# Pooled attention, then a gated product: x @ w1 and x @ w2 by one level of Strassen's scheme, in two passes over the batches

## The chip, the cores and the metric

The kernel runs on one core of one Trainium2 chip. A core has TensorE (PE, the matrix unit, with its weight loads shown apart as PEld), VectorE (DVE), ScalarE (ACT), GpSimd (POOL) and SyncE (SP), which here issues all DMAs. Each engine works through its own instructions in order and waits for others at semaphores. The metric is the device time of one execution in microseconds (us); lower is better. Matmuls write to PSUM, which has eight banks of 128 x 512 float32.

## What is computed

```python
def _attn_ref(q, k, v):                     # q, k, v: 8 batches, 8 heads, 576 rows, 64 columns, float32
    k_p = k.reshape(B, H, 72, 8, D).mean(axis=3)
    v_p = v.reshape(B, H, 72, 8, D).mean(axis=3)
    scores = matmul(q, k_p.T) / sqrt(D)
    attn = softmax(scores)
    return matmul(attn, v_p)

def _moe_ref(x, w1, w2, w3, w_out):         # x: 4608 x 512 (heads side by side); w1, w2: 512 x 1024
    a = x @ w1                              # w3: 1024 x 1024; w_out: 1024 x 512; the weights are float64
    b = x @ w2
    return (a * b @ w3) @ w_out             # 4608 x 512, float32
```

Both kernels compute w3 @ w_out first, once, call it W (1024 x 512), and then (a * b) @ W for the tokens.

## The kernel before

The order of all work is written out by hand. Each piece is entered in a plan with a step number (`at(kind, k, fn, ...)`), the plan is sorted by step and, inside a step, by kind (L loads, P work after a matmul, M matmuls of the large products, A matmuls of the attention), and the pieces are issued in that order. Since every engine runs in order, the plan is also the order on each engine's queue.

Weights come as float64, read as pairs of int32. `high` (ACT) and `low`, `conv_b` (DVE) put a float32 together from the two words; `conv_c` sets its sign with ACT's Sign and a product on POOL. Every operand of a large product is split in a rounded part and the rest, `hi` and `lo` (`split`: ACT copies, DVE or POOL subtracts), and each product is done in three passes, hi*hi, hi*lo and lo*hi (`PASSES`).

*Prologue.* For 16 blocks of w3 and 8 of w_out: load, convert, transpose w3 on PE (`w_turn`), split, and multiply (`w_mm`, L571) into W. Beside the second half of this stand the attention of the first tokens and, behind it, the conversion of w1 and w2 in 16 blocks of 512 x 128 (`w12_conv` to `w12_split`), which go into the cells that w3 and w_out leave free.

*Main loop.* Tokens go in 12 chunks of 384 (m). For each of 8 column blocks j of w1 and w2: `a_mm` and `b_mm`, each 12 matmuls (4 blocks of the inner dimension by 3 passes, L510) of 384 columns, `a_post` (ACT copies a from PSUM), `b_post` (DVE multiplies a by b, L530; ACT rounds, L531), `g_lo` (DVE, the rest, L536), and one j later `out_mm`, 9 matmuls of 512 columns (L545) that add to three banks o0 to o2. After the last j `out_post` copies the three banks and stores them.

*Attention.* While chunk m is multiplied, chunk m + 1 goes through attention, spread over m's steps: `load_q` and DVE's transpose (L287); k and v pooled over 8 rows by three additions on POOL (`pool_tree`, L347 to L349); scores (`s_mm`, L389); minima and exponentials (`soft1`: L405, L407, L410 and L411, or the form with ACT's accumulator, L415); normalisation (`soft2`, L424 to L427); copies of the columns left over beyond 128 (`soft3`, L436, L438); PE transposes of the weights (L449, L459) and their splits (L471, L472); the product with v (`av_mm`, L484 to L487), and its split into x's two parts (`av_post`, L495, L496).

PSUM: one bank each for a and b, three for the output, three for attention (`patt`).

Of the kernel before, what the change touches and what calls it, by code (L numbers as in the profile page):

```python
# [29 lines left out]
):  # L30

# [27 lines left out]
    xp = ctx.enter_context(tc.tile_pool(name="xp", bufs=2))  # L59
    p1 = ctx.enter_context(tc.tile_pool(name="p1", bufs=1))  # L60
    p2 = ctx.enter_context(tc.tile_pool(name="p2", bufs=2))
    stp = ctx.enter_context(tc.tile_pool(name="stp", bufs=4))
    osp = ctx.enter_context(tc.tile_pool(name="osp", bufs=3))
    pacc = ctx.enter_context(tc.tile_pool(name="pacc", bufs=1, space=PSUM))
    patt = ctx.enter_context(tc.tile_pool(name="patt", bufs=3, space=PSUM))


    ident = cp.tile([P, P], F32, name="ident")
    kbd = [cp.tile([P, NPR, 2 * KP], F32, name=f"kbd{i}") for i in range(2)]
    vbd = [[cp.tile([P, NPR, P], F32R, name=f"vbd{i}_{s}") for s in range(2)] for i in range(2)]  # L70
    VR = [cp.tile([P, NPR, P], F32R, name=f"VR{i}") for i in range(2)]
# [10 lines left out]
    for i in range(2):  # L82
        nc.gpsimd.memset(kbd[i], 0.0)
        for s in range(2):
            nc.gpsimd.memset(vbd[i][s].bitcast(F32), 0.0)
        nc.gpsimd.memset(VR[i].bitcast(F32), 0.0)
# [3 lines left out]

    def raw_cell(i):
        return cp.tile([P, 1024], I32, tag=f"c{i}", name="raw")

    def hl_cell(i):
        t = cp.tile([P, 2, 512], F32R, tag=f"c{i}", name="hl")
        return t[:, 0], t[:, 1]

    def W_cell(s, i, dt):
        return cp.tile([P, DM], dt, tag=f"W{s}_{i}", name="Wc")

    raw, w3t, wo, w12, W = {}, {}, {}, {}, {}
    FREED = (8, 0, 9, 1, 10, 2, 11, 3, 12, 4, 13, 5, 14, 6, 15, 7)
    w1r, w2r, w3r, wor = (w.bitcast(I32) for w in (moe_w1, moe_w2, moe_w3, moe_w_out))
    stage = {}
    NS = 2 * NJ

    def st_tile(shape):  # L110
        return stp.tile(shape, F32, tag="st", name="st")

    def load_wo(j):
        raw["wo", j] = raw_cell(8 + j)
        nc.sync.dma_start(out=raw["wo", j], in_=wor[j * P:(j + 1) * P, :])

    def load_w3(s):
        h, j = divmod(s, NJ)
        raw["w3", s] = raw_cell(s % 4)
# [4 lines left out]
    def load_w12(j, w):  # L124
        raw["w12", j, w] = raw_cell(FREED[2 * j + w])
        nc.sync.dma_start(
            out=raw["w12", j, w].rearrange("p (k c) -> p k c", k=NK),
            in_=(w1r, w2r)[w][:, 2 * j * P:2 * (j + 1) * P].rearrange("(k p) c -> p k c", p=P))
# [11 lines left out]
    def conv_a(c, r, z):  # L140
        high(c, z)
        low(c, r)

    def conv_b(r, z):
# [3 lines left out]

    def conv_c(r, z):
        nc.scalar.activation(out=z, in_=z, func=AF.Sign)  # L150
        nc.gpsimd.tensor_tensor(out=f(r), in0=f(r), in1=z, op=ALU.mult)

    def split(src, hi, lo, eng=nc.vector):
        nc.scalar.copy(out=hi, in_=src)
        eng.tensor_tensor(out=lo, in0=src, in1=f(hi), op=ALU.subtract)  # L155

    def w_tiles(s):
        if s == 0:
            stage["wt"] = [t[:, i] for t, x in (
                (p1.tile([P, x, 512], I32, tag=tag, name="wt"), x)  # L160
                for tag, x in (("PTh", 3), ("PTl", 3), ("PTr", 1))) for i in range(x)]
        if s < NJ:
            stage["wo", s] = stage["wt"][s % 4], f(stage["wt"][4 + s % 3])
        stage["w3", s] = W_cell(0, 4 + s % 4, I32), W_cell(1, 4 + s % 4, F32)

    def w_block(v):
# [10 lines left out]
        if old:  # L177
            s = v - 2
            nc.vector.tensor_tensor(out=wo[s][1], in0=f(stage["wo", s][0]), in1=f(wo[s][0]), op=ALU.subtract)  # L179
        if new:  # L180
            if v > 0:
                low(raw["wo", v], ro)
# [5 lines left out]
        if new:  # L188
            conv_c(r3, z3)
            if v == 0:  # L190
                low(raw["wo", v], ro)
# [543 lines left out]
```

## Time and profile before

| what | value |
|---|---|
| median of 3 runs | 829.68 us (829.64 to 829.82) |
| the profiled execution | 831.34 us, span 829.4 us, mean granted TensorE clock 0.974 |
| DMA moved | 62.63 MB: 52.43 MB read from HBM, 9.44 MB written |
| first matmul of the main loop | at 107.3 us |
| chunk 1 begins, last chunk begins | at 186.3 us and 773.0 us |

The profile is that of one execution. "Busy" is the time in which an engine had an instruction in it; rows of instructions name the line of the kernel, the engine, the operation and the tiles (out<-in). The span is cut in 40 slices on the page, and each digit is a slice's busy share in tenths. Two waits are the longest of those on PE's products: ACT for a (L520) 160.5 us and DVE for b (L530) 122.4 us; in both the waiting engine is not the one that sets the pace.

### The profile page before, as it was taken

The page shows a single profiled execution, that of the slowest core. Times are in us where ns is not written, and L with a number is a line of the kernel's source. Part 1 is how long each engine was busy: PE and PEld are TensorE (multiplying, and loading weights), DVE is VectorE, ACT ScalarE, POOL GpSimd, SP SyncE. Part 2 cuts the span into 40 slices and gives each one's busy share as a digit, 9 for nine tenths or more (in the row PEclk, how much of TensorE's full clock was granted, in tenths as well). Part 3 has the DMA queues.
Part 4 walks back from the last instruction along what each step waited for, and adds up shares of the span by engine and source line. Part 5 has one row for each costly group of instructions (what it writes and reads, how often), then busy time and mean ns, then how long its engine had stood idle before and what let it go on. Part 6 is the DMA issues. An engine that isn't in the chain of part 4 may idle for free.

```text
span 829.4 us, 11726 instructions
## 1 busy us (share of the span) xinstructions
PE 785.1 (95%) x4320; PEld 726.7 (88%) x4320; DVE 460.9 (56%) x881; ACT 304.6 (37%) x759; POOL 255.9 (31%) x274
## 2 busy tenths in 40 slices
PE   6787788699999999999999999999999999999998
PEld 5466677699999999999999999999999999999997
DVE  7997899856537337446345356365373374462112
ACT  5756656633224323323234233232243233232111
POOL 5586679630700810205203603007008102000000
PEclk8979988999999999999999999999999999999999
DMA  9896882004403403017014230044034030100101
GB/s 330 205 207 160 243 196 56 1 1 105 106 1 88 106 19 75 1 39 151 22 46 88 77 76 1 1 105 106 2 84 109 20 76 1 39 1 1 39 0 39
DMA packets 113160, 62.63 MB, mean 76 GB/s; under 512 B 80208, under 2 KB 96848, under 8 KB 113104
## 3 DMA queue, kind: packets, MB, share of 16 engines
q1 hardware_dynamic: 113104, 61.89, 29.7%
q8 instruction: 34, 0.56, 0.3%
q14 instruction: 22, 0.18, 0.1%
HBM read 52.43 MB, written 9.44 MB: 75 GB/s over the span
## 4 chain that ended last, share of the span: by engine, by line
PE 80%; DVE 9%; DMA 5%; issue 4%; ACT 2%; SPq 1%; DVEq 0%
PE o L545 23%; PE a L510 23%; PE b L510 23%; PE att L389 4%; DMA raw<-in_moe_w_dram 3%; PE att L449 2%; DVE Wc L138 2%; PE att L486 1%; PE att L485 1%; PE att L487 1%; PE att L484 1%; PE att L459 1%; DMA raw<-in_moe_w_out_dram 1%; ACT E L415 1%; DVE R L438 1%
## 5 line engine op out<-in xcount | busy, mean ns | idle before, releaser
L510 PE MATMUL a<-xT,hl 128*128 128x384 f32 x1152 | 223.3, 342 | 0.0
L510 PE MATMUL b<-xT,hl 128*128 128x384 f32 x1152 | 221.9, 340 | 0.0
L510 PEld LDWEIGHTS a<-xT,hl 128*128 128x128 f32 x1152 | 205.2, 191 | 5.1 <-POOL hl L155 0.3
L510 PEld LDWEIGHTS b<-xT,hl 128*128 128x128 f32 x1152 | 200.6, 190 | 0.0
L545 PE MATMUL o<-Wc,gh 128*128 128x512 f32 x576 | 183.6, 400 | 0.0
L530 DVE TENSOR_TENSOR a<-b,a 128x384 f32<-128x384 f32 x96 | 53.1, 553 | 122.4 <-PE b L510 122.4
L545 PEld LDWEIGHTS o<-Wc,gh 128*128 128x128 f32 x576 | 105.1, 189 | 17.3
L545 PE MATMUL o<-Wc,gl 128*128 128x512 f32 x288 | 114.0, 396 | 0.0
L520 ACT COPY a<-a 128x384 f32<-128x384 f32 x96 | 46.0, 479 | 179.5 <-PE a L510 160.5
L347 POOL TENSOR_TENSOR st<-st 72x512 f32<-72x512 f32 (+1 forms) x53 | 74.3, 1402 | 121.8 <-DMA st<-in_k_dram 121.1
L531 ACT CAST gh<-a 128x384 fp32r<-128x384 f32 x96 | 49.1, 512 | 148.5 <-DVE a L530 148.3
L360 POOL TENSOR_TENSOR vbd<-vm,vbd 64x256 fp32r<-64x256 f32 x16 | 13.8, 862 | 248.4 <-ACT vbd L359 245.0
L536 DVE TENSOR_TENSOR gl<-a,gh 128x384 fp32r<-128x384 f32 x96 | 60.3, 628 | 36.2 <-ACT gh L531 35.8
L496 DVE TENSOR_TENSOR xT<-att,xT 128x384 fp32r<-128x384 f32 x48 | 26.7, 557 | 75.1 <-ACT xT L495 75.1
L545 PEld LDWEIGHTS o<-Wc,gl 128*128 128x128 f32 x288 | 54.1, 188 | 12.5
L411 DVE TENSOR_REDUCE sm<-E 128x4 f32<-128x288 f32 (+1 forms) x70 | 31.6, 451 | 46.3 <-ACT E L410 46.3
L389 PE MATMUL att<-kbd,qT 128*128 128x144 f32 (+1 forms) x320 | 53.3, 290 | 1.2 <-ACT E L415 1.2
L571 PE MATMUL o<-hl 128*128 128x512 f32 x144 | 45.2, 452 | 9.1 <-DVE hl L179 8.9
L405 DVE TENSOR_REDUCE mx<-att 128x4 f32<-128x288 f32 (+1 forms) x80 | 35.9, 449 | 30.3 <-PE att L389 30.3
L410 ACT ACTIVATE E<-E 128x288 f32<-128x288 f32 (+1 forms) x70 | 31.1, 445 | 54.3 <-DVE E L407 54.2
L389 PEld LDWEIGHTS att<-kbd,qT 128*128 128x128 f32 (+1 forms) x320 | 47.5, 182 | 2.3 <-ACT E L415 1.7
L571 PEld LDWEIGHTS o<-hl 128*128 128x128 f32 x144 | 30.1, 216 | 17.8 <-DVE hl L179 11.3
(90 smaller groups left out, 927.8 us busy)
## 6 DMA issues: line engine op xcount, KB each, us to landing
raw<-in_moe_w_dram SPq DMA_DIRECT2D x32, 512.0 KB
st<-in_k_dram SPq DMA_DIRECT2D x32, 288.0 KB
out_dram<-ob SPq DMA_DIRECT2D x35, 256.0 KB
st<-in_v_dram SPq DMA_DIRECT2D x32, 256.0 KB
qs<-in_q_dram SPq DMA_DIRECT2D x128, 48.0 KB
raw<-in_moe_w_out_dram SPq DMA_DIRECT2D x8, 512.0 KB
st<-in_v_dram SPq DMA_DIRECT2D x64, 64.0 KB
qs<-in_q_dram SPq DMA_DIRECT2D x128, 24.0 KB
```

Source lines behind the costliest of these rows:

```text
L347: nc.gpsimd.tensor_tensor(out=t[:, :, 0:4], in0=t[:, :, 0:4], in1=t[:, :, 4:8], op=ALU.add)
L389: nc.tensor.matmul(out=ps[:nt, 2 * KP * j:2 * KP * (j + 1)], lhsT=qT[n][:, pr, off:off + nt], rhs=kbd[b % 2][:, pr], start=True, stop=True,)
L405: nc.vector.tensor_reduce(out=mx[:nt, hs], in_=sv, axis=AX.X, op=ALU.min)
L410: nc.scalar.activation(out=E[:nt, hs], in_=E[:nt, hs], func=AF.Exp, scale=-1.0)
L411: nc.vector.reduce_sum(out=sm[:nt, hs], in_=E[:nt, hs], axis=AX.X)
L510: nc.tensor.matmul(out=o, lhsT=w12[j, w][sw][:, kt * P:(kt + 1) * P], rhs=x[sx][:, kt], start=(i == 0), stop=(i == 3 * NK - 1))
L520: nc.scalar.copy(out=a, in_=gt[m, j][:, :CH])
L530: nc.vector.tensor_tensor(out=g, in0=ps[:, :CH], in1=g, op=ALU.mult)
L531: nc.scalar.copy(out=gh, in_=g)
L536: nc.vector.tensor_tensor(out=gl, in0=g, in1=f(gh), op=ALU.subtract)
L545: nc.tensor.matmul(out=oacc[m][t], lhsT=(gh, gl)[sg][:, c], rhs=W[j][sw], start=(j == 0 and i == 0), stop=(j == NJ - 1 and i == 2))
L571: nc.tensor.matmul(out=wacc[h][it], lhsT=w3t[s][sa][:, it * P:(it + 1) * P], rhs=wo[j][sb], start=(j == 0 and i == 0), stop=(j == NJ - 1 a ...
```

## The change

Nearly all functions of the kernel are rewritten; the attention's arithmetic, the three passes and the prologue's w3 @ w_out are kept.

*Seven products for eight.* x of one batch (576 tokens, transposed: 512 x 576) is cut in 2 x 2 blocks (256 x 288), and so is each quarter of the columns: in a pass, w1 and w2 have 512 columns each, as two quarters of 256, so that `qq` runs over (w1, w2) twice. One level of the Strassen-Winograd scheme gives the 2 x 2 result from 7 products of blocks. Each is a group of 6 matmuls of 288 columns (`grp_mm`). Before, a batch's same quarter was 8 such products.

*Sums of weights*, once in a pass (`w12_sums`, `w12_split`): four sums per quarter on DVE, and splits of all seven operands.

*Sums of x*, once for each batch and pass (`x_sum1`, `x_sum2`: four subtractions on DVE of 128 x 576; `x_split`: seven splits, ACT and DVE).

*Sums of products* (`grp_post`): ACT copies the first group; DVE adds the others from PSUM, seven additions in a quarter. For w1 the four results go to the tile `g`; for w2 they are added up in small tiles and POOL multiplies them into `g`.

*Two passes.* Iterations 0 to 7 are the batches with the first half of the columns, 8 to 15 the same with the second half. x of each batch is kept in DRAM (`xd`, `x_store`, `x_load`), partial outputs too (`pd`); in the second pass `out_post` adds them. Half of W waits in DRAM as well (`wbd`). The conversion of w1's and w2's second half lies in iteration 7.

*Output.* `out_mm` now comes after the four quarters, in tiles of 128 tokens, two halves each. Odd batches have 5 tiles, even ones 4: the last 64 tokens of an even batch stay in `g` and go with the next (`SHIFT`).

*Steps.* An iteration has 24: groups in the first 14, two a step; from step 13 on x's sums and splits for the next iteration, the splits of g, and the output halves from step 14.

*Other edits.* Attention goes by batch (5 tiles of up to 128 tokens) and x is left unsplit by it (`av_post` only copies). `conv_c` is gone; `conv_b` has a second DVE instruction for the sign. All pooling of k and all splits of w1 and w2 have one engine (POOL and DVE). kbd, vbd and VR have one copy instead of two. PSUM: four banks for groups (`pset`), four for attention and output (`patt`).

```diff
     def conv_b(r, z):
...
         nc.vector.scalar_tensor_tensor(
             out=r, in0=z.bitcast(I32), scalar=3, in1=r, op0=ALU.logical_shift_left, op1=ALU.bitwise_or)
-
-    def conv_c(r, z):
-        nc.scalar.activation(out=z, in_=z, func=AF.Sign)
-        nc.gpsimd.tensor_tensor(out=f(r), in0=f(r), in1=z, op=ALU.mult)
+        nc.vector.scalar_tensor_tensor(
+            out=r, in0=z.bitcast(I32), scalar=-2 ** 31, in1=r, op0=ALU.bitwise_and, op1=ALU.bitwise_or)
...
+    def w12_sums(ph, qq):
...
+        add(s1, a21, a22)
+        sub(s2, s1, a11)
+        sub(s3, a11, a21)
+        sub(s4, a12, s2)
...
+    def x_sum1(i):
+        t = stage["xs", i] = [p2.tile([P, 2, HS], F32, tag="qs", name="xs") for _ in range(2)]
+        sub(t[0], xb(i, 0, 1), xb(i, 0, 0))
+        sub(t[1], xb(i, 1, 1), t[0])
+
+    def x_sum2(i):
+
+        t = stage["xs", i]
+        sub(t[0], xb(i, 1, 1), xb(i, 0, 1))
+        sub(t[1], xb(i, 1, 0), t[1])
+
+    def x_split(i, n):
+        t = p1.tile([P, 2, 2, HS], F32R, tag=f"xo{XN.index(n)}", name="xo")
+        xo[i, n] = t[:, 0], t[:, 1]
...
+        split(src, *xo[i, n])
...
+    GROUPS = (("A11", "B11"), ("S2", "T2"), ("S1", "T1"), ("S3", "T3"),
+              ("A12", "B21"), ("S4", "B22"), ("A22", "T4"))
...
+    def grp_mm(i, qq, n):
...
+        wn, xn = GROUPS[n]
+        ps = acc[i, qq, n] = pset.tile([P, 512], F32, tag=f"p{(7 * qq + n) % 4}", name="ps")
+        w, x = sw[i // B, qq, wn], xo[i, xn]
+        for j, (kt, (a, b)) in enumerate((kt, ps) for kt in range(2) for ps in PASSES):
+            nc.tensor.matmul(out=ps[:, :HS], lhsT=w[a][:, kt * P:(kt + 1) * P], rhs=x[b][:, kt],
+                             start=(j == 0), stop=(j == 5))
+
+    def grp_post(i, qq, n):
+
+        o = acc.pop((i, qq, n))[:, :HS]
+        w2 = qq % 2
+
+        def res(jj, t2, u, into):
+            d = quad(i, qq, jj, t2)
+            if w2:
+                add(tmp[into], u, o)
+                mul(d, d, tmp[into], nc.gpsimd)
+            else:
+                add(d, u, o)
+
+        if n == 0:
...
+            nc.scalar.copy(out=tmp["m1"], in_=o)
+        elif n == 1:
+            add(tmp["u2"], tmp["m1"], o)
+        elif n == 2:
+            add(tmp["u4"], tmp["u2"], o)
+        elif n == 3:
+            add(tmp["u3"], tmp["u2"], o)
+            res(1, 1, tmp["u4"], "u5")
+        elif n == 4:
+            res(0, 0, tmp["m1"], "m1")
+        elif n == 5:
+            res(0, 1, tmp["u4"], "u4")
+        else:
+            res(1, 0, tmp["u3"], "u3")
...
+    def out_post(i, t):
         ob = osp.tile([P, DM], F32, tag="ob", name="ob")
...
+        ps = oacc.pop((i, t))
+        if i < B:
+            if t % 2:
+                nc.vector.tensor_copy(out=ob, in_=ps)
             else:
...
+                nc.scalar.copy(out=ob, in_=ps)
+            nc.sync.dma_start(out=pd[tile_no(i, t)], in_=ob)
+            return
+        add(ob, part.pop((i, t)), ps)
...
+    for i in range(NIT):
+        m0 = M0 + IT * i
+        for qq in range(4):
+            for n in range(7):
+                g = 7 * qq + n
+                k = m0 + g // 2
+                at("M", k + 0.1 * (g % 2), grp_mm, i, qq, n)
+                at("P", k + 1 + 0.01 * (g % 2), grp_post, i, qq, n)
+        nt = len(out_tiles(i))
+        order = [(0, 0), (1, 0), (0, 1), (1, 1)] + [(t, h) for t in range(2, nt) for h in range(2)]
+        for x, (t, h) in enumerate(order):
+            k = m0 + OUT0 + x
+            at("M", k, out_mm, i, t, h)
+            if t < 2:
+                at("P", k - 1 + 0.13 if h == 0 else k + 0.13, g_split, i, t, slice(2 * h, 2 * h + 2))
+            elif h == 0:
+                at("P", k - 0.87, g_split, i, t, slice(0, 4))
+            if h:
+                at("P", k + 1.05, out_post, i, t)
+            if i >= B and h == 0:
+                at("L", k - 3, part_load, i, t)
+        if i + 1 < NIT:
+            plan_x(i + 1, m0 + OUT0 - 1)
+        if i + 1 < B:
+            at("L", m0 + OUT0 + 8, x_store, i + 1)
+        if B <= i + 1 < NIT:
+            at("L", m0 - 2, x_load, i + 1)
```

More of the change, by code (lines that the diff above doesn't have):

```diff
@@ new lines, in w12_split @@
+    def w12_split(ph, qq):
+        own = [cell(i, [P, 2, 512], F32R, "sw") for i in OWN[qq]]
+        if qq % 2 == 0:
+            stage["both"] = cell(BOTH[qq // 2], [P, 2, 2, 256], F32R, "sw")
+        s12, r0, s34, a22 = stage.pop(("sums", ph, qq))
+        for i, (t, src) in enumerate(zip(own, (r0, s12, s34))):
+            for o in range(2):
+                c = slice(256 * o, 256 * o + 256)
+                sw[ph, qq, NAMES[2 * i + o]] = t[:, 0, c], t[:, 1, c]
+            split(src, t[:, 0], t[:, 1])
+        both = stage["both"][:, :, qq % 2]
+        sw[ph, qq, "A22"] = both[:, 0], both[:, 1]
+        split(a22, *sw[ph, qq, "A22"])
@@ new lines, with rows, soft_act, load_q @@
+    NT = (S + P - 1) // P
+    def rows(t):
+        return min(P, S - t * P)
+    def soft_act(n, t):
+        return n == 0 or t in (1, 3)
+    qT, km, vm = {}, {}, {}
+    def load_q(n, pr):
+        t = stage["q", n, pr] = p2.tile([P, S // 32, 32], F32, tag="qs", name="qs")
+        for par in range(2):
+            for db in range(2):
+                g = 2 * par + db
+                nc.sync.dma_start(
+                    out=t[32 * g:32 * g + 32],
+                    in_=q[n, 2 * pr + par, :, 32 * db:32 * db + 32].rearrange("(n t) e -> t n e", t=32))
@@ L357, in prep_v2 @@
         r = slice(64 * par, 64 * par + 64)
-        hi, lo = (vbd[b % 2][s][r, :, D * par:D * par + D] for s in range(2))
-        nc.scalar.copy(out=hi, in_=vm[b][r])
-        nc.gpsimd.tensor_tensor(out=lo, in0=vm[b][r], in1=f(hi), op=ALU.subtract)
+        hi, lo = (vbd[s][r, :, D * par:D * par + D] for s in range(2))
+        split(vm[b][r], hi, lo, nc.gpsimd)
     def prep_vr(b):
@@ L471, in pt_post @@
[L471 to L472 removed]
+        hi, lo = (x[:, :, t * P:t * P + nt] for x in PT[n][:2])
+        split(pv[:, :, :nt], hi, lo)
     def ptr_post(n, t):
[L475 to L488 removed]
@@ L550, in out_post @@
-    def out_post(m, t):
-        ob = osp.tile([P, DM], F32, tag="ob", name="ob")
-        r0 = m * CH + t * P
-        last = m == NCH - 1 and t == 2
-        for i in range(2 if last else 1):
-            c = slice(i * DM // 2, (i + 1) * DM // 2) if last else slice(0, DM)
-            if t == 1 or i == 1:
-                nc.vector.tensor_copy(out=ob[:, c], in_=oacc[m][t][:, c])
-            else:
-                nc.scalar.copy(out=ob[:, c], in_=oacc[m][t][:, c])
-            nc.sync.dma_start(out=out[r0:r0 + P, c], in_=ob[:, c])
+        nt = rows(t)
@@ new lines, in out_tiles, with g_split @@
+    def out_tiles(i):
+        b = i % B
+        r = [(SHIFT + P * t, [(b * S + SHIFT + P * t, P)]) for t in range(4)]
+        if b % 2 == 0:
+            return r
+        return [(0, [((b - 1) * S, SHIFT), (b * S, SHIFT)])] + [(c + SHIFT, x) for c, x in r]
+    oacc, part = {}, {}
+    def g_split(i, t, js):
+        if js.start == 0:
+            G[i, t] = [p2.tile([P, 4, P], F32R, tag=tag, name=tag) for tag in ("gh", "gl")]
+        c = out_tiles(i)[t][0]
+        h, l = G[i, t]
+        split(G["g"][:, js, c:c + P], h[:, js], l[:, js])
@@ new lines, in out_mm, with tile_no, part_load @@
+    def out_mm(i, t, half):
+        if half == 0:
+            oacc[i, t] = bank()
+        for j in (2 * half, 2 * half + 1):
+            for n, (a, b) in enumerate(PASSES):
+                nc.tensor.matmul(
+                    out=oacc[i, t], lhsT=G[i, t][a][:, j], rhs=W[i // B, j][b],
+                    start=(j == 0 and n == 0), stop=(j == 3 and n == 2))
+    def tile_no(i, t):
+        return 9 * (i % B // 2) + 4 * (i % 2) + t
+    def part_load(i, t):
+        if "part" not in stage:
+            stage["part"] = p1.tile([P, 4, DM], F32, tag="PTh", name="part")
+        part[i, t] = stage["part"][:, t % 4]
+        nc.sync.dma_start(out=part[i, t], in_=pd[tile_no(i, t)])
```

606 lines of the change are left out of this document (283 added, 323 removed).

## The prediction

> **What bounds the kernel now.** I read the page's busy shares first, then its 40 slices, then the stretches of the program one by one, then TensorE's timeline and the groups of instructions by shape.
>
> ```profile
> span 829.4 us, 11726 instructions
> PE 785.1 (95%) x4320; PEld 726.7 (88%) x4320; DVE 460.9 (56%) x881; ACT 304.6 (37%) x759; POOL 255.9 (31%) x274
> PE   6787788699999999999999999999999999999998
> DVE  7997899856537337446345356365373374462112
> PE 80%; DVE 9%; DMA 5%; issue 4%; ACT 2%; SPq 1%; DVEq 0%
> ```
>
> The kernel has two parts. Over the first nine slices VectorE (DVE) is as full as anything; from the ninth on TensorE (PE) never rests, and VectorE is near half. The cuts below are the first product with w1 (107.3), the starts of chunk 1 (186.3) and of the last chunk (773).
>
> ```profile
> 0.00:107.30 107.30, 80.57 (x367) 64.44 (x368) 93.77 (x128) 66.07 (x162) 70.85 (x70) 0.87 0.86 231
> 107.30:186.30 79.00, 65.40 (x349) 60.37 (x348) 66.03 (x92) 42.34 (x117) 53.30 (x43) 0.91 0.24 53
> 186.30:773.00 586.70, 586.70 (x3337) 553.30 (x3336) 290.50 (x643) 186.23 (x461) 131.79 (x162) 1.00 0.23 55
> 773.00:829.40 56.40, 52.48 (x274) 48.57 (x272) 10.65 (x19) 9.98 (x20) 0.00 (x0) 0.98 0.08 28
> ```
>
> Columns: stretch, length, then busy PE, weight loads, DVE, ACT, POOL, then clock, DMA share, GB/s. Ten chunks take 586.7 us, all of it PE at clock 1.00: 58.67 each. DVE does 29.05 us of work in each, POOL 13.2. So a saved matmul is worth its time there, and added DVE work is free as long as it stays under PE's time. That limit is what this prediction turns on.
>
> **What PE gains.** The rows give the rate at three widths, and the price of attention work slipped in between:
>
> ```profile
> 699.39 0.27 PE L484 MATMUL att<-PTh,vbd 128*128 128x192 f32 x1
> ...
> 699.83 2.27 PE L510 MATMUL a<-xT,hl 128*128 128x384 f32 x12
> ...
> 724.41 0.65 PE L389 MATMUL att<-kbd,qT 128*128 128x144 f32 x4
> 724.81 2.34 PE L510 MATMUL b<-xT,hl 128*128 128x384 f32 x12
> 726.99 0.65 PE L389 MATMUL att<-kbd,qT 128*128 128x144 f32 x4
> 729.57 0.60 PE L449 MATMUL att<-ident,E 128*128 128x128 f32 x4
> 730.00 0.38 PE L459 MATMUL att<-ident,R 128*128 128x128 f32 x2
> 730.14 2.35 PE L510 MATMUL a<-xT,hl 128*128 128x384 f32 x12
> ...
> 804.39 2.27 PE L510 MATMUL a<-xT,hl 128*128 128x384 f32 x12
> 806.50 2.24 PE L510 MATMUL b<-xT,hl 128*128 128x384 f32 x12
> 808.58 0.62 PE L545 MATMUL o<-Wc,gh 128*128 128x512 f32 x2
> 810.67 1.58 PE L510 MATMUL a<-xT,hl 128*128 128x384 f32 x8
> ```
>
> From start to start: 24 matmuls of 384 columns take 4.19 us, 0.1746 each; 9 of 512 take 2.09, 0.2322 each; four of 192 (L484 to L487) take 0.44, 0.11 each, which lies above the line through the other two (0.088), so a floor shows there. 288 columns are not in the trace; they lie between 0.11 and 0.1746, and the line of the two wide ones gives 0.131. I take that.
>
> - Before, one j costs 6.28 us (804.39 to 810.67), a chunk 50.24, twelve 602.9. Attention adds 58.67 - 50.24 = 8.43 to a chunk, eleven times 92.7. Together 695.6.
> - After, there are 16 iterations (8 batches, 2 passes) of 28 groups of 6 matmuls: 0.79 a group, 22.1 an iteration. The output has 4 or 5 tiles of 12 matmuls of 512, 2.79 each, 12.5 on average. One iteration is 34.6 us.
> - Attention of one batch: 10 score halves at 0.49 (0.40, and 0.10 that the next group loses: 2.18 for 2.08), 5 tiles of transposes at 0.65, 8 products at 4 x 0.131, 0.3 for k: 12.6 us, seven times in the loop.
> - After in all: 16 x 34.6 + 7 x 12.6 = 641.8. PE's work falls by 54 us.
>
> A rule of the Trainium skill would price this differently: TensorE: Matmul & The Clock Gate, section Back-to-back issue gap, gives columns/2.4 GHz plus 2.5 ns, an estimated 0.1225 us at 288. The trace disagrees at 384, where that rule gives 0.1625 and the rows 0.1746. By the rule the 2688 group matmuls would be 24 us cheaper.
>
> **What the other engines pay.** Rows of groups by shape (busy us, mean ns):
>
> ```profile
> L407 DVE TENSOR_TENSOR E<-att,mx 128x288 f32<-128x288 f32 x42 | 19.2, 457 | 1.4
> L427 DVE TENSOR_TENSOR E<-E,sm 128x576 f32<-128x576 f32 x24 | 19.1, 797 | 0.8
> L427 DVE TENSOR_TENSOR E<-E,sm 96x576 f32<-96x576 f32 x16 | 15.0, 936 | 0.5
> L405 DVE TENSOR_REDUCE mx<-att 128x4 f32<-128x288 f32 x48 | 21.6, 451 | 21.6 <-PE att L389 21.6
> L472 DVE TENSOR_TENSOR PTl<-att,PTh 128x512 fp32r<-128x512 f32 x24 | 16.5, 689 | 10.7 <-ACT PTh L471 10.5
> L287 DVE STREAM_TRANSPOSE qT<-qs 128x384 f32<-128x384 f32 x48 | 27.2, 567 | 0.0
> L146 DVE SCALAR_TENSOR_TENSOR wt<-wt 128x512 int32<-128x512 int32 x8 | 5.4, 680 | 0.3 <-ACT wt L133 0.3
> L426 DVE RECIPROCAL sm<-sm 128x8 f32<-128x8 f32 x24 | 4.9, 203 | 0.8
> L347 POOL TENSOR_TENSOR st<-st 128x512 f32<-128x512 f32 x24 | 32.5, 1355 | 0.5
> L348 POOL TENSOR_TENSOR st<-st 128x256 f32<-128x256 f32 x24 | 19.2, 801 | 1.9
> L349 POOL TENSOR_TENSOR km<-st 72x128 f32<-72x128 f32 x29 | 16.4, 566 | 2.3
> ```
>
> Back to back, a VectorE instruction starts before the row of the one ahead of it ends:
>
> ```profile
> 161.94 0.68 DVE L146 SCALAR_TENSOR_TENSOR wb<-wb 128x512 int32<-128x512 int32 x1
> 162.54 0.55 DVE L530 TENSOR_TENSOR a<-b,a 128x384 f32<-128x384 f32 x1
> 163.01 0.44 DVE L405 TENSOR_REDUCE mx<-att 96x4 f32<-96x288 f32 x1
> 163.49 0.45 DVE L407 TENSOR_TENSOR E<-att,mx 96x288 f32<-96x288 f32 x1
> ```
>
> Starts lie 0.60, 0.47 and 0.48 apart. An independent one costs its row less 0.08 on a full queue; one that needs the one ahead (L407 after L405) pays 0.04 on top. The Trainium skill (VectorE: DVE Perf Modes, The DRAIN you can't avoid) has the next instruction wait until the pipe is empty; the trace shows no such full wait. With whole durations the sum below would be 6 us more in each attention iteration.
>
> One iteration of the first pass with attention, on DVE:
> - group sums: 7 additions a quarter from PSUM (u2, u4, u3 and four results), 28 x (0.457 - 0.08) = 10.5;
> - the combinations of x and their splits: 4 + 7 instructions of 576 columns at 0.758 (L427's median, below) - 0.08 = 7.4;
> - splits of g, 0.61 for 512 columns and 0.34 for 256: 2.9; two copies of partial results: 1.2;
> - attention: 4 transposes of 576 columns 2.75; 10 minima and 6 subtractions 6.7; 3 sums of 576 columns 2.0; 5 normalisations (0.20 + 0.24 + 0.68) 5.5; 10 small subtractions 1.45; 5 splits 2.8: 21.2.
>
> Sum 43.2, against PE's 47.2 for the same iteration and DVE's 1.5 x 29.05 = 43.6 for a batch in 88 us before. So DVE gets as much work in roughly half the time. POOL has 7 pooling trees at about 2.75 (L347, L348, L349), 4 of small work, and 8 new products of 288 columns at about 0.87 (between L348 and L347): 30 us of some 52, 58%, where before it was 131.79 of 586.7, 22%. That costs DVE time:
>
> ```profile
> L427 DVE TENSOR_TENSOR E<-E,sm x40: 753/758/1700, 73.1 to 739.8; 128x576 f32<-128x576 f32 x24, 96x576 f32<-96x576 f32 x16
> L536 DVE TENSOR_TENSOR gl<-a,gh x96: 514/558/2014, 118.1 to 822.5; 128x384 fp32r<-128x384 f32 x96
> L146 DVE SCALAR_TENSOR_TENSOR wb<-wb 128x512 int32<-128x512 int32 x16 | 20.8, 1301 | 0.9 <-ACT wb L133 0.8
> ```
>
> Minimum, median, maximum: two SBUF inputs usually cost 0.758 and at worst 1.700. The 40 take 34.1 us, 12% over the median's 30.3; L146 beside POOL's conversions averages 1.301 where it costs 0.680 without them. Scaled from 22% to 58%, 17.2 us of such work an iteration grows by a third, 6 us: 49. Bounds: 0, and 17 if everything doubles as L146 did.
>
> That is above PE's 47.2, and the work is not even. The output's ten steps also hold the x work, g's splits, copies and two softmax tiles: 18 us on DVE, 21.5 with contention, against PE's 15.5 (12.5, two tiles of scores, one of transposes). The 14 group steps hold the group sums, q's transposes and three softmax tiles: DVE 27, PE 32. Were each part bound by its own engine, it would be 53.6; four PSUM banks let PE run about 3 us ahead. I take 52. ScalarE did 18.6 a chunk, 28 a batch (186.23 over ten chunks); with x's and g's splits for those it loses it stays near that, and hides.
>
> **The sum.**
> - Prologue, on DVE: 24 weight conversions at 1.64 (the sign is now a second L146, 0.68, instead of ACT and POOL) 39.4, their splits 14.4, six conversions of w1/w2 with sums and splits 21, attention 0 16.2, x 7.4, the rest 4: 103, with contention 9, first data 4: 116; DVE was 93.77 of 107.3 busy before, with less POOL beside it now I take 93%: 126 (118 to 138). Before, the stall-free equivalent is 829.4 - 695.6 - 6 of tail = 128. So nothing is gained.
> - Iteration 0: 49, 0.4 of the next attention 8.5, the last quarter of the weights 7: 65 (58 to 70).
> - Iterations 1 to 5: 52 each, 260 (48 to 60 each).
> - Iteration 6 holds half an attention and falls to PE: 44.
> - Iteration 7: 22.2 as above, and the second half of w1/w2: 8 conversions 13.2, 16 sums 6.2, splits 8.7, contention 2.5: 53.
> - Second pass, 8 times: PE's 22.1 for groups; output 12.5 on PE, 13.0 on DVE (7.4, 2.9, additions of partial results 2.7); and a handoff of 2, since the last quarter's sum, POOL's product and both splits stand behind x work while PE has 2.8 of other output: 37 (35.5 to 39). Sum 296, less 2 for the last, which prepares no x.
> - Tail 6.
>
> 126 + 65 + 260 + 44 + 53 + 294 + 6 = 848 of span, 18 over the 829.4 of before. The profiled execution took 831.34 in all, 1.9 more than its span and 0.2% over the median of 829.68; the two about cancel, so 848 stands for the median too.
>
> New transfers (x 1.18 MB out and in, partial results alike) are put at nothing: DMA is 0.23 busy in the loop, and a read of x is issued 15 steps before its use. Without that cover each read costs 5 us (at the 231 GB/s of the first row), 40 in all. SP issues in order, so a partial result that waits for its copy holds back k and v loads, and POOL behind them; that belongs to the slower rival.
>
> **The rivals.**
> 1. Faster: DVE keeps under PE. If contention stays below 4 us an iteration, every iteration is PE's 47.5: 118 + 60 + 5 x 47.5 + 44 + 50 + 8 x 35.5 - 2 + 6 = 798. For it: 43.2 is below 47.2, and L407, with an input in PSUM, averages 0.457 and 0.45 alone (163.49), so the group sums should not stretch. Against: it needs DVE over 90% busy in order, with ACT and POOL between its steps. It decides at about 50 us an iteration, with the second pass at 36; below that the change wins.
> 2. Slower still: POOL blocks DVE for whole instructions. 37 instructions with only SBUF operands meet POOL 58% of the time and wait half of 1.36: 15 us, so 58 to 60 an iteration, 75 for the first, 39 in the second pass: 130 + 75 + 5 x 59 + 48 + 58 + 310 + 6 = 922 at the full price, 885 at half. L536's 2.014 (0.558 plus one L347) speaks for it, its median against it. The Trainium skill states just that (SBUF — State Buffer, Who interferes with whom): the later of the two fully blocks.
> 3. The change doesn't do what it says: 288 columns cost what 384 do. 2688 x 0.043 = 116 us more on PE, 58 of them in the second pass and on the path; in the first PE's 47 become 54, 2 over my 52: some 920. The 192 rows speak against it.
>
> **How the numbers follow.** Within 0.2% (1.7 us) is what a measurement of this kernel cannot tell from no change. Mine 0.50, its own range 822 to 878; the first rival 0.21 (798 to 828); between them within 0.2%: 0.04; the second 0.22 (878 to 925); the third 0.03. Faster 0.21, same 0.04, slower 0.75. The range 808 to 900 leaves out the lower part of the first rival and the upper part of the second.
>
> **What would show it.** Group matmuls 0.131 apart, and DVE over 90% busy between about 126 and 545 us with PE below 95%, then PE full again with DVE near 80%. L427's mean above 1.0 us would show the contention. Wrong if iterations 1 to 5 take PE's 47 us, or if PE waits for POOL's products or for x's read instead of DVE.

## The result, and the profile after

The changed kernel takes 1083.27 us (median of 4 runs, 1082.66 to 1083.32) where the kernel before takes 829.75 on the same chip: a ratio of 1.304 (1.3025 to 1.3059). It is 30% slower. The prediction had the sign right and missed the size by far: 848 was forecast, with 900 as the upper end.

The page of the kernel after: length, busy time of the engines, TensorE, VectorE and the granted clock in 40 slices, and the chain that ended last by engine.

```profile
span 1081.4 us, 13558 instructions
PE 840.3 (78%) x4704; PEld 722.0 (67%) x4704; DVE 761.9 (70%) x1415; ACT 358.1 (33%) x1033; POOL 309.8 (29%) x354
PE   7467436667868878788796896759789898898898
DVE  7756795885786867867778773995775765756654
PEclk9868768778989889799798997869899898898989
PE 39%; DVE 38%; ACT 11%; issue 5%; DMA 4%; POOL 2%; SPq 2%; DVEq 0%; ACTq 0%; POOLq 0%
```

Before, TensorE's line was a row of nines from the ninth slice on, and the chain was 80% TensorE. Now no engine stays full: TensorE is busy 78% of the span and VectorE 70%, and the chain goes to and fro between them, 39% and 38%. So look at the stages: prologue, iteration 0, iterations 1 to 5, 6, 7, and the second pass with the tail, then without its last iteration. Columns: stretch, length, then busy PE, weight loads, DVE, ACT, POOL, then clock, DMA share, GB/s.

```profile
0.00:160.30 160.30, 90.71 (x422) 72.78 (x423) 118.38 (x202) 68.21 (x195) 44.70 (x55) 0.80 0.59 162
160.30:262.40 102.10, 68.89 (x352) 59.38 (x352) 72.51 (x137) 38.91 (x130) 37.84 (x44) 0.78 0.25 68
262.40:612.30 349.90, 281.74 (x1648) 242.41 (x1647) 264.57 (x504) 140.24 (x466) 159.92 (x175) 0.89 0.38 91
612.30:665.60 53.30, 47.56 (x285) 41.19 (x284) 35.17 (x75) 20.75 (x62) 6.56 (x8) 0.90 0.07 26
665.60:737.00 71.40, 47.38 (x229) 39.70 (x228) 54.86 (x105) 22.73 (x44) 7.61 (x8) 0.78 0.38 127
737.00:1081.40 344.40, 303.96 (x1777) 266.58 (x1775) 216.42 (x393) 67.24 (x138) 53.16 (x64) 0.92 0.23 79
737.00:1040.40 303.40, 267.16 (x1550) 233.32 (x1549) 195.89 (x352) 62.46 (x127) 46.57 (x56) 0.92 0.24 80
```

| stage | predicted | measured | more |
|---|---|---|---|
| prologue | 126 | 160.3 | 34 |
| iteration 0 | 65 | 102.1 | 37 |
| iterations 1 to 5 | 260 (52 each) | 349.9 (70.0 each) | 90 |
| iterations 6, 7 | 44, 53 | 53.3, 71.4 | 9, 18 |
| second pass and tail | 300 | 344.4 | 44 |

Every term is short, and in each stage the two loaded engines have gaps. In iterations 1 to 5 VectorE's work is 264.57 / 5 = 52.9 us each, where the forecast had 49, and TensorE's busy time 56.3, where it had 47.2; the iteration takes 70.0. Part of TensorE's excess goes with the granted clock, 0.89 here and 1.00 in the chunks before; how much is not separated. An iteration falls into a part with the groups and a part with the output. Here are one of the first pass (402.10) and one of the second (866.10), groups first:

```profile
402.10:438.40 36.30, 32.33 (x236) 30.25 (x235) 27.32 (x63) 13.47 (x48) 13.05 (x17) 1.00 0.55 102
438.40:472.30 33.90, 24.46 (x102) 18.15 (x101) 26.38 (x41) 14.84 (x46) 19.02 (x20) 0.80 0.22 81
866.10:888.40 22.30, 22.30 (x169) 22.30 (x168) 12.85 (x29) 2.48 (x6) 4.26 (x6) 1.00 0.29 109
888.40:911.60 23.20, 18.55 (x62) 13.12 (x62) 15.60 (x23) 6.42 (x12) 2.32 (x3) 0.78 0.29 88
```

In the second pass the groups run as a row of matmuls with nothing between: 168 of them in 22.30 us, 0.133 each. What the change promised for TensorE is there in full. The output part lasts 19 to 23 us where TensorE has 11 to 14 of work, and in the first pass 32 to 34 where the forecast gave it 15.5. The output parts hold most of the loss: the x work of the next iteration and g's splits stand there on VectorE. What TensorE waits for in the iteration at 402.10, the two longest (us in total, times, longest us), where `gh` is the rounded part of g, from ScalarE, and `gl` the rest, from VectorE:

```profile
PE att L604 <- DVE gl L94: 4.7, 4, 1.9
PE att L604 <- ACT gh L151: 4.4, 4, 2.1
```

All of these lie in the output part, and they are 9.1 of TensorE's 13.8 us of waits in that iteration.

What the instructions cost, from the groups by shape (busy us, mean ns), and the same instructions one by one in the first pass's output part, on DVE and on POOL:

```profile
L546 PE MATMUL ps<-xo,sw 128*128 128x288 f32 x2688 | 392.8, 305 | 13.7 <-DVE u L97 9.0
L97 DVE TENSOR_TENSOR u<-u,ps 128x288 f32<-128x288 f32 x224 | 94.6, 449 | 32.7 <-PE ps L546 31.6
L94 DVE TENSOR_TENSOR xo<-xs,xo 128x576 fp32r<-128x576 f32 x64 | 61.0, 952 | 10.5 <-ACT xo L151 8.4
L94 DVE TENSOR_TENSOR xs<-x 128x576 f32<-128x576 f32 x32 | 39.0, 1219 | 0.6
L100 DVE TENSOR_TENSOR E<-E,sm 128x576 f32<-128x576 f32 x32 | 24.6, 770 | 1.1
```

```profile
445.25 1.72 DVE L94 TENSOR_TENSOR xs<-x 128x576 f32<-128x576 f32 x1
...
448.10 1.00 DVE L94 TENSOR_TENSOR xo<-xs,xo 128x576 fp32r<-128x576 f32 x1
449.02 1.83 DVE L94 TENSOR_TENSOR xo<-x,xo 128x576 fp32r<-128x576 f32 x1
450.77 0.94 DVE L94 TENSOR_TENSOR gl<-g,gh 128x256 fp32r<-128x256 f32 x1
```

```profile
444.57 2.99 POOL L97 TENSOR_TENSOR st<-st 128x512 f32<-128x512 f32 x2
448.45 2.99 POOL L97 TENSOR_TENSOR st<-st 128x512 f32<-128x512 f32 x2
```

The x work lies right beside POOL's pooling trees: 1.0 to 1.83 where the forecast took 0.758. The softmax's product on full tiles (L100, once L427), most of which lies elsewhere, is at 0.770. The additions that read PSUM (L97) are not stretched at all: the 25 of them that overlap the trees' additions take at most 0.455. Contention is a matter of place, and an average over the iteration by POOL's busy share could not see it. This is the second rival's mechanism. Whether it is also the second rival's *time* is what the experiments ask.

### The profile page after: what moved, and what is told of

It reads as the page before. It is cut to its first block, busy times and chain, and to the rows that moved or that the text cites. A ratio compares the mean times of both kernels' runs of the same rounds, so it can differ in the third digit from the quotient of the medians.

```text
span 1081.4 us, 13558 instructions
## 1 busy us (share of the span) xinstructions
PE 840.3 (78%) x4704; PEld 722.0 (67%) x4704; DVE 761.9 (70%) x1415; ACT 358.1 (33%) x1033; POOL 309.8 (29%) x354
## 2 busy tenths in 40 slices
DMA packets 124869, 102.60 MB, mean 95 GB/s; under 512 B 79744, under 2 KB 96128, under 8 KB 122752
## 4 chain that ended last, share of the span: by engine, by line
PE 39%; DVE 38%; ACT 11%; issue 5%; DMA 4%; POOL 2%; SPq 2%; DVEq 0%; ACTq 0%; POOLq 0%
PE ps L546 22%; PE att L604 13%; DVE xs L94 6%; DVE xo L94 6%; ACT E L425 4%; DVE gl L94 4%; DVE u L97 3%; ACT xo L151 2%; DVE mx L418 2%; POOL st L97 2%; DVE wr L147 2%; DVE wr L145 1%; DVE E L100 1%; DVE PTl L94 1%; DVE sw L94 1%
## 5 line engine op out<-in xcount | busy, mean ns | idle before, releaser
L546 PE MATMUL ps<-xo,sw 128*128 128x288 f32 x2688 | 392.8, 305 | 13.7 <-DVE u L97 9.0
L546 PEld LDWEIGHTS ps<-xo,sw 128*128 128x128 f32 x2688 | 377.6, 196 | 20.1 <-DVE u L97 9.9
L604 PE MATMUL att<-W,gh 128*128 128x512 f32 x576 | 212.9, 455 | 60.8 <-ACT gh L151 60.8
L100 POOL TENSOR_TENSOR g<-g,u 128x288 f32<-128x288 f32 x96 | 79.3, 840 | 541.1 <-DVE u L97 541.1
L604 PEld LDWEIGHTS att<-W,gh 128*128 128x128 f32 x576 | 119.4, 218 | 97.7 <-ACT gh L151 77.9
L604 PE MATMUL att<-W,gl 128*128 128x512 f32 x288 | 132.7, 461 | 46.1 <-DVE gl L94 46.1
L97 POOL TENSOR_TENSOR st<-st 72x512 f32<-72x512 f32 (+1 forms) x112 | 136.2, 1216 | 87.1 <-DMA st<-in_k_dram 52.1
L97 DVE TENSOR_TENSOR u<-u,ps 128x288 f32<-128x288 f32 x224 | 94.6, 449 | 32.7 <-PE ps L546 31.6
L604 PEld LDWEIGHTS att<-W,gl 128*128 128x128 f32 x288 | 61.5, 214 | 83.6 <-DVE gl L94 71.0
L94 DVE TENSOR_TENSOR gl<-g,gh 128x256 fp32r<-128x256 f32 (+1 forms) x104 | 71.6, 699 | 29.8 <-ACT gh L151 29.5
L97 DVE TENSOR_TENSOR u<-m,ps 128x288 f32<-128x288 f32 x64 | 29.0, 453 | 61.1 <-PE ps L546 51.6
L151 ACT CAST gh<-g 128x256 fp32r<-128x256 f32 (+1 forms) x104 | 49.5, 486 | 42.4 <-PE att L604 36.6
L97 DVE TENSOR_TENSOR ob<-part,att 128x512 f32<-128x512 f32 x36 | 24.8, 688 | 49.3 <-PE att L604 49.2
```

Of the source, the lines that this page charges most:

```text
L94: eng.tensor_tensor(out=out, in0=a, in1=b, op=ALU.subtract)
L97: eng.tensor_tensor(out=out, in0=a, in1=b, op=ALU.add)
L100: eng.tensor_tensor(out=out, in0=a, in1=b, op=ALU.mult)
L546: nc.tensor.matmul(out=ps[:, :HS], lhsT=w[a][:, kt * P:(kt + 1) * P], rhs=x[b][:, kt], start=(j == 0), stop=(j == 5))
L604: nc.tensor.matmul(out=oacc[i, t], lhsT=G[i, t][a][:, j], rhs=W[i // B, j][b], start=(j == 0 and n == 0), stop=(j == 3 and n == 2))
```

## The experiments

Two readings run through all of them. The first is a sum of work: POOL's trees stretch VectorE's instructions, VectorE is the bound, and time falls with its work. The second is a chain: TensorE, VectorE and ScalarE wait for each other in order (products to VectorE's sums, to g's or x's splits on ScalarE and VectorE, back to TensorE), so their times partly add, and time falls only if a step is taken out of the chain or moved ahead in its queue. All times below are of one execution beside the kernel before on the same chip (830 us) unless an interval is given; two executions of the last version differ by 2.9 us, so small differences are read from the stages and not from the total. "Each" means iterations 1 to 5, which some of the expectations call 2 to 6.

**The x work, later.** The x work stood before g's splits from one step ahead of the output; here it begins 4.2 steps later.

```
-            plan_x(i + 1, m0 + OUT0 - 1)
+            plan_x(i + 1, m0 + OUT0 + 3.2)
```

> x's sums and splits for the next iteration are moved 4.2 steps later in the plan, behind the splits of g for the first two output tiles. Theory of order (x work stands ahead of g's splits on VectorE's queue, PE waits for them and its clock falls): second-pass iterations from 43.3 us to 37, first-pass ones (2 to 6) from 70 to about 62; about 980 us in all. Theory of load (the first pass is as long as VectorE's and POOL's work with its stretching makes it, wherever it stands): second pass the same gain of 45 us, first pass stays at 70; about 1038. If the later splits make the next groups wait instead: 1083.

Measured: 1039.74 us, 1.252 (1.2485 to 1.2557) times the time before. Iterations 1 to 5, the second pass up to its last iteration, and one group:

```profile
262.30:606.30 344.00, 281.99 (x1649) 242.88 (x1647) 237.66 (x504) 139.98 (x466) 146.13 (x175) 0.92 0.39 93
723.30:997.50 274.20, 254.60 (x1550) 228.56 (x1549) 185.90 (x352) 62.20 (x127) 46.48 (x56) 0.98 0.26 86
```

```profile
L94 DVE TENSOR_TENSOR xs<-x 128x576 f32<-128x576 f32 x32 | 25.2, 788 | 0.6
```

Most of the stretching is gone (788 ns instead of 1219), and VectorE's work in iterations 1 to 5 falls by 27 us, 5.4 each. Their time falls by 5.9 us in all, 1.2 each. The total is the one that the theory of load gave (1038), but that theory had the stretching stay wherever the x work stands, and it went. That speaks against a sum of work in the first pass: 5.4 us less on what should be the bound, and little more than a fifth of it comes back. What the stretching costs by itself this does not show, since the later x work also comes later for the next groups (those parts last 36 to 39 us here, 36 to 38 before). In the second pass, where no trees run and the work falls by only 10 us in seven iterations, each falls from 43.3 to 39.2: there g's splits no longer wait behind the x work.

**No x work but the first.** All iterations use the first batch's x.

```
-        w, x = sw[i // B, qq, wn], xo[i, xn]
+        w, x = sw[i // B, qq, wn], xo[0, xn]
...
-            plan_x(i + 1, m0 + OUT0 - 1)
```

> x's sums and splits are left out for all batches but the first, whose operands every batch uses. Theory of order: second pass 35.5 us an iteration, as in the last one, which prepares no x; first pass about 60, close to what x_late gives; about 940 in all. Theory of load: the first pass falls by more than x_late's, by the 10 to 13 us that the work takes, to 57 to 60, while x_late's stays near 70.

Measured: 967.32 us.

```profile
252.60:565.60 313.00, 267.13 (x1649) 234.09 (x1647) 202.43 (x450) 119.42 (x431) 143.44 (x175) 0.96 0.43 102
674.20:924.20 250.00, 245.41 (x1550) 225.15 (x1549) 135.38 (x275) 33.67 (x78) 46.50 (x56) 1.00 0.29 98
```

Without it the second pass is TensorE's, 245.41 of 250.00 at clock 1.00, 35.7 us each, as expected: nearly its whole excess over TensorE's 34.6 is the x work. The first pass falls to 62.6 each, which is above what either theory gave: 7.4 less for 12.4 us less on VectorE, and still 15 us too many.

**No pooling trees.** The first two additions of `pool_tree` are left out.

> Two of the three additions of each pooling tree on POOL are left out (k and v are then pooled over two rows only). Theory of contention (POOL holds VectorE up): VectorE's x splits fall from 1.0 to about 0.76 us each, first-pass iterations from 70 to 62 to 64, prologue 5 us less; about 1020 to 1035. Theory of order: the rows get shorter, but an iteration loses only 2 to 4 us: about 1055 to 1065.

Measured: 1029.54 us; 63.9 each, with the output parts at 29.5 and 27.4, and VectorE's work at 47.0 each:

```profile
240.30:559.60 319.30, 273.68 (x1649) 235.67 (x1647) 235.12 (x504) 141.15 (x466) 77.22 (x105) 0.94 0.40 100
```

6.1 us less each, 12.5 in iteration 0, and the first group comes 9.6 us earlier, at 150.7. That is the time that the theory of contention gave, though the x rows fell less than it said (`xo<-xs,xo` from 0.952 to 0.889 on average, not to 0.76). VectorE loses 5.9 each by this, hardly other than when x came later (5.4), yet time falls five times as much. The trees may also cost time by their place on POOL, and in k's way to the scores, and not only by stretching VectorE; how these divide is not separated.

**No softmax but the first.** After batch 0 one exponential per half stands for the softmax; `soft2` returns.

> For batches 1 to 7 the minima, subtractions, sums and normalisations of softmax are left out; one exponential for four heads stays. VectorE loses about 16 us an iteration, ScalarE 6; PE's work stays. Theory of order and chains: 70 falls by more than VectorE's idle 16 us would need, to 54 to 57. If x's work and the pooling trees alone hold the output up: 65 to 68.

Measured: 1008.11 us; 60.1 each:

```profile
237.80:538.20 300.40, 260.07 (x1649) 233.53 (x1648) 198.71 (x333) 120.96 (x326) 156.52 (x177) 0.91 0.45 106
```

That lies between the two forecasts (54 to 57, 65 to 68). The group part is 31.3 us in each iteration: TensorE's own work there, for which the forecast had 32. The output part stays at 27 to 30. Iteration 0 falls by 25, to 77.3.

**All three left out.** The edits of the last three together.

> no_x, no_trees and no_soft together: x's sums and splits only for batch 0, one of three pooling additions, and no minima, sums and normalisations for batches 1 to 7. Alone they took 7.4, 6.1 and 9.9 us from the 70.0 of iterations 2 to 6. Theory that VectorE's queue sets the first pass and PE is the floor: the three add up, to PE's 47 us (its 47.2 of work). If other round trips (groups and their sums, transposes and their splits) hold PE as well: 52 to 55. About 880 in all, second pass 35.7.

Measured: 858.74 us; 49.8 each:

```profile
209.70:458.90 249.20, 247.88 (x1649) 226.54 (x1647) 123.65 (x278) 99.30 (x291) 65.92 (x106) 0.99 0.54 128
```

TensorE is busy 247.88 of 249.20 us: here is its floor, near the 47 of the forecast. Singly the three gave 7.4, 6.1 and 9.9, a sum of 23.4; together they give 20.2, cut off by that floor. Two lessons. The jobs of VectorE and POOL, though they would fit beside TensorE's work by their sum (52.9 in 70), lie in part end to end with it: with 28 us of VectorE's work gone, the other waits that were feared (52 to 55) do not show. And even with all three gone the change is 28 us slower than the kernel before.

**The softmax moved into the group part.** Scores and softmax one part later, where VectorE had 9 us free and POOL is quieter.

```
-            plan_att(n, [k - 8 + 3.4 * t for t in range(NT)], 4,
-                     [[k + 6 + p for p in range(4)], [k + 11 + 0.5 * p for p in range(4)]])
+            plan_att(n, [k - 1 + 1.6 * t for t in range(NT)], 3.5,
+                     [[k + 7 + 0.5 * p for p in range(4)], [k + 10 + 0.5 * p for p in range(4)]])
```

> For batches 2 to 7 the attention gets the steps that batch 1 has: all five softmax tiles lie beside the groups of one iteration and none beside its output. Theory of order (each engine's queue holds softmax ahead of g's splits in the output's steps): the output's part of a first-pass iteration falls from 33.5 to about 25, the groups' part grows from 37 to 42, an iteration 70 to 67. Theory of chains (a softmax tile takes its round trips between VectorE, ScalarE and PE wherever it stands): 70 or more; with all five tiles in one stretch 72 to 75.

Measured: 1097.56 us, slower; 72.9 each. The output parts fall from 32–34 to 28–31, the group parts rise from 37 to 43.5. This is what the theory of chains forecast (72 to 75): the softmax takes its time wherever it stands.

**The softmax on VectorE alone.** ScalarE's accumulating form is not used: VectorE sums instead.

```
-        return n == 0 or t in (1, 3)
+        return False
```

> All exponentials take the form with one ACT instruction for four heads and the sum on VectorE (before: all tiles of batch 0 and two of five of the others had one ACT instruction and one accumulator read per head). It takes about 7 us from ACT and adds 3.3 us to VectorE in an iteration. Theory of round trips (g's and m1's copies wait on ACT's queue behind 16 exponentials, and VectorE behind them): first-pass iterations 70 to 65, first matmul group 10 to 20 us earlier; about 1040. Theory of load: iterations 3 us longer, 1100.

Measured: 1077.73 us; 69.3 each, although VectorE's work rises from 52.9 to 56.0:

```profile
260.80:607.20 346.40, 278.60 (x1649) 240.97 (x1647) 280.00 (x534) 124.23 (x326) 158.33 (x175) 0.90 0.39 92
```

My 1040 missed, and so did the 1100 of the theory of load; the first group came 1.3 us earlier, not 10 to 20. ScalarE's form is not what holds things up. But 3.1 us more work on the supposed bound costs nothing, which is against a sum of VectorE's work once more. It does not show that added work is free: ScalarE loses 3.2 us each by the same edit (140.24 to 124.23 in five iterations), so the two may cancel in a chain that holds both.

**Matmuls on nothing in the output part.** In the second pass 14 and 8 products with the identity are put in TensorE's gaps.

```
+            if i >= B and x in (1, 2):
+                at("M", k + 0.01, warm, 14 if x == 1 else 8)
```

> In the second pass 14 transposes that nobody reads are put behind the second output half and 8 behind the third, where PE waited 1.3 to 1.6 us at a time for g's splits and then ran 3 to 4 us at half clock. Theory of order alone: PE waits as long, now filled; second-pass iterations 43.3 or up to 2 longer. If the fallen clock adds to the path by itself: the half-rate stretch goes, 43.3 to about 41 an iteration, 1065 in all.

The gaps in question, on TensorE's timeline of the kernel after:

```profile
889.18 0.62 PE L604 MATMUL att<-W,gh 128*128 128x512 f32 x2
889.64 0.40 PE L604 MATMUL att<-W,gl 128*128 128x512 f32 x1
891.53 0.74 PE L604 MATMUL att<-W,gh 128*128 128x512 f32 x2 [1.50 <-ACT gh L151]
893.53 0.79 PE L604 MATMUL att<-W,gl 128*128 128x512 f32 x1 [1.27 <-DVE gl L94]
894.13 1.05 PE L604 MATMUL att<-W,gh 128*128 128x512 f32 x2
894.98 0.63 PE L604 MATMUL att<-W,gl 128*128 128x512 f32 x1
897.23 1.22 PE L604 MATMUL att<-W,gh 128*128 128x512 f32 x2 [1.63 <-ACT gh L151]
```

After two waits a pair of matmuls takes 0.85 us from start to start (894.13 to 894.98) where it took 0.46 (889.18 to 889.64). The granted clock was 1.00 from 891.5 to 893.0 and 0.50 from 894.1 to 895.6. With the fillers, the same part:

```profile
891.39 0.62 PE L604 MATMUL att<-W,gh 128*128 128x512 f32 x2
891.85 0.39 PE L604 MATMUL att<-W,gl 128*128 128x512 f32 x1
892.09 1.69 PE L199 MATMUL att<-ident 128*128 128x128 f32 x14
894.77 0.73 PE L604 MATMUL att<-W,gh 128*128 128x512 f32 x2 [0.99 <-ACT gh L151]
...
896.02 0.63 PE L604 MATMUL att<-W,gh 128*128 128x512 f32 x2
896.49 0.40 PE L604 MATMUL att<-W,gl 128*128 128x512 f32 x1
```

The rate stays full: 0.46 ahead of the fillers (891.39 to 891.85) and 0.47 behind them. Over the first seven iterations of the pass the clock is 0.98 instead of 0.92:

```profile
736.60:1034.30 297.70, 272.44 (x1703) 246.03 (x1702) 195.89 (x352) 62.48 (x127) 46.60 (x56) 0.98 0.24 82
```

Their time falls from 43.3 to 42.5 each, 0.8, and the whole takes 1078.65. So the lower clock adds little to the path of the second pass, and many of the matmuls that it slows are followed by another wait anyway. The first pass was not tried.

**The trees, earlier.** `plan_kv` of batches 3 to 7 starts 7.5 steps sooner; nothing is left out.

```
-plan_kv(n, k - (17.5 if n == 2 else 19.5), 1.75, ...
+plan_kv(n, k - (17.5 if n == 2 else 27), 1.5, ...
```

> The pooling of k and v for batches 3 to 7 stands 7.5 steps earlier, beside the groups, whose sums read PSUM, and not beside the output, where x's sums and splits read SBUF alone. Nothing is left out. Theory of contention (VectorE's SBUF-only work and POOL's block each other where they meet): x's rows from 1.0 to 1.2 us to about 0.8, the output's part of iterations 3 to 6 from 33 to 28, an iteration 64 to 66; about 1055 in all. Theory of POOL's load (it takes the same wherever it stands): 69 to 71.

Measured: 1065.18 us; 67.5 each, between the two theories, the output parts at 30 and 27, the groups at 36 to 40. VectorE's work is 49.5 each: 3.4 less work gives 2.5 less time, which is far more for its size than when x came later.

**The prologue.** First, k, v and q of batch 0 are loaded four steps later, so that w3's second half comes sooner. Then VectorE is relieved: the sign goes back to ScalarE and POOL.

```
-plan_kv(0, K0 - 13.5, ...)   plan_q(0, K0 - 11, 1.5, K0 - 9, 1.5)
+plan_kv(0, K0 - 9.5, ...)    plan_q(0, K0 - 7, 1.5, K0 - 5, 1.5)
```

> The loads of batch 0's q, k and v and the work on them stand 4 steps later in the plan, behind three more loads of w3. Theory of the first loads (SyncE's queue puts 16 q, 4 k and 4 v loads ahead of w3's second half, whose first product comes at 72 us): w3's second half starts near 60 and the first group at 160 comes at 145 to 150. Theory of load (VectorE is what fills the prologue): 158 to 162.

```
-        nc.vector.scalar_tensor_tensor(out=r, in0=z.bitcast(I32), scalar=-2 ** 31, in1=r, ...)
+        nc.scalar.activation(out=z, in_=z, func=AF.Sign)
+        nc.gpsimd.tensor_tensor(out=f(r), in0=f(r), in1=z, op=ALU.mult)
```

> One edit is undone: the sign of a converted weight comes from ScalarE's Sign and a product on POOL again, in place of the second VectorE instruction (0.69 us, 30 times before the first group, 8 times in iteration 7). Theory of load (VectorE's work sets the prologue): the first group starts at 145 to 150 instead of 160, iteration 7 falls from 71 to 67. Theory of chains (each conversion passes through several queues in turn, and VectorE idles 26% of the prologue): two more steps in each chain and POOL beside it again, 160 to 168, iteration 7 at 71 or more.

In the chain of the kernel after, this stands ahead of the product with w3's second half (first and last of eight issues of v's loads at SP's queue):

```profile
57.19 0.66 SPq L367
...
61.21 0.62 SPq L367
62.44 5.08 DMA raw<-in_moe_w_dram
...
72.40 5.27 PE ps L642 x12
```

With the loads later that product starts at 63.20 instead of 72.40:

```profile
63.20 4.88 PE ps L642 x12
```

but the first group of the main loop comes only at 154.0 instead of 160.3, short of the 145 to 150 of the theory of the first loads, and the whole takes 1076.64. With the sign moved, VectorE does 102.39 us in the prologue instead of 118.38, and the prologue is 7 us *longer*, as the theory of chains said (160 to 168; iteration 7 takes 74.4); the whole takes 1091.21:

```profile
0.00:167.20 167.20, 97.67 (x423) 77.79 (x423) 102.39 (x172) 84.50 (x225) 82.24 (x85) 0.79 0.58 155
```

So neither VectorE's load nor that queue alone sets the prologue. VectorE is 74% busy in the kernel after and 61% here, with a conversion that passes through two more engines. The pooling trees have a share in it (150.7 without them). What else holds it is not settled.

**Three moves at once.** Trees earlier, x later, k, v and q of batch 0 later: the best version that computes everything.

> trees_early, x_late and kvq_late together, nothing left out. Alone x_late took 41 us and kvq_late 6; with trees_early's 25 that adds to about 1010. If x_late and trees_early free the same wait (x's stretched work ahead of g's splits), less: 1025.

Measured: 1019.62 us (1018.18 to 1021.05), 1.228 (1.2237 to 1.232) times the time before; the first group at 152.5, 66.6 each, the second pass 39.3 each. Alone the three moves saved 43.5, 18.1 and 6.6 us, together 63.7: they nearly add up.

```profile
250.60:583.50 332.90, 275.10 (x1647) 239.87 (x1646) 235.86 (x505) 140.15 (x466) 142.98 (x174) 0.92 0.37 93
```

VectorE's work is down to 47.2 each, at mean rows of 0.79, and the iteration is still 19 us longer than that and 17 longer than TensorE's floor (49.8 above). No version beats the kernel before.

## Why the prediction was right in sign and wrong in size

*Right.* The rate of the groups: 0.133 against 0.131, so that the third rival (no saving) is out. VectorE's work, nearly: 52.9 an iteration against 49, 27.3 in the group part against 27, 118 in the prologue against 112 with contention. TensorE's work: 31.3 in the group part against 32. ScalarE's: 28.0, as forecast, though its steps stand in the chain. The new transfers, put at nothing: 102.60 MB move instead of 62.63, and DMA is 4% of the chain (5% before). The prediction's rule against the change, the Trainium skill's "Who interferes with whom" in SBUF — State Buffer (two-SBUF-input operations of VectorE contend with POOL's reads), agrees with the rows: 1.219 and 0.952 on average in this kernel, where much of the x work lies beside the trees, 0.788 with x later, and 0.449 for those that read PSUM. How much of it was on the path stays open: moving the x work or the trees apart gave 1.2 and 2.5 of the 18 us by which an iteration missed, both moves 3.4, and leaving most of the trees out 6.1.

*Wrong, the step that failed.* "Were each part bound by its own engine, it would be 53.6; four PSUM banks let PE run about 3 us ahead. I take 52." Likewise "I take 93%" for the prologue. The working took the larger of two engines' sums in each part, as if the smaller ran freely beside it, and for the first pass it had no term for a wait between them. Measured, VectorE is busy 74% in the prologue, 71% in iteration 0, 76% in iterations 1 to 5 and 65% between 737.0 and 1040.4. The runs put waits in order, a chain, in that place. TensorE waits 9.1 us an iteration for g's splits alone, and whole jobs of VectorE that are taken out give back most of their length as time (no x 7.4 for 12.4, no softmax 9.9 for 13.2), although VectorE had 17 us free. The same amount of VectorE's work is worth more or less by where it stands: x later gives 1.2 us for 5.4, trees earlier 2.5 for 3.4. "DVE over 90% busy between about 126 and 545 us with PE below 95%" was the sign that was named for the forecast; PE is below 95%, DVE is not over 90%, and this says that the bound is neither.

*Mis-sized: the second pass.* "A handoff of 2" was to stand behind x work. The mechanism is right and shown (no x: 35.7 us; x later: 39.2; as is: 43.3), but by the working's own terms (22.1 for groups and 13.0 for the output) it is 43.3 - 35.1 = 8.2, not 2. VectorE's 13.0 us of output work was held against TensorE's 12.5 as a sum, though g's splits stand behind x work on VectorE's queue and the output's matmuls can't begin without them.

*Missing: iteration 0.* With 37 over, it is the worst of the single iterations. It was summed as 49 + 8.5 + 7 of VectorE work, and VectorE did 72.51 in 102.10. The softmax of two batches is most of it (25 us less without), and without the trees it falls by 12.5; the two may overlap.

*The rivals.* The second, 885 to 922, was nearest, and named the right rows, but it would also have been a sum of VectorE's work. The range ended at 900 because all cases were sums.

*Left open.* Whether the chain is long by the engines' round trips or by too few buffers: a third buffer for g's splits was not tried. How much of the first pass's loss is the trees' stretching of VectorE, how much their place on POOL, and how much TensorE's lower clock. And what, beside the order of the loads and the trees, makes up the 34 us of the prologue.

## What to carry to other kernels

A free engine's share of the time is no offer of that much time: VectorE was 50% busy in the ten chunks before and TensorE never waited for it, and with 300 us more of VectorE's work (761.9 for 460.9) to save a forecast 54 of TensorE's, the two waited for each other. Where two engines with nearly equal work hand results to and fro, estimate by the queue and not by the larger sum: for each handoff write down what stands ahead of it on the engine that produces it, and add that. No run here tests this as a way to forecast; it is what this forecast lacked.

## What the runs showed of the hardware

In the output part at 888.40 no wait of TensorE is longer than 1.63 us, and yet the granted clock falls from 1.00 to 0.50 and a pair of matmuls of 512 columns goes from 0.46 to 0.85. The Trainium skill (TensorE: Matmul & The Clock Gate, The HAM clock gate) puts a whole idle window of about 3.4 us before the lower clock; here a row of shorter waits, two within 4 us, came before it. Those two alone do not decide it: in the run with the fillers the same two (1.49 and 1.28) were followed by a pair at 0.46, before the fillers of that part had run.

The second surprise is how exact the divide is between kinds of VectorE operands: beside the same pooling additions on POOL, two inputs in SBUF cost up to 1.83 instead of 0.76, and one input in PSUM costs at most 0.455, with a mean of 0.449 anywhere.
